# A banded attention and FFN kernel: one issue order for both phases, and shared DMA semaphores taken in written order

## The chip, the cores and the metric

One core of a Trainium2 chip runs the kernel. The metric is the device time of one execution in microseconds (us), the median of several executions. Engines are named as the profile names them: PE is TensorE (PEld its weight loads), DVE is VectorE, ACT is ScalarE, POOL is GpSimd, SP is SyncE; ACTq and SPq are the transfers that ACT and SP issue.

## What is computed

The reference, cut to what matters (q, k and v are 8 batches x 8 heads x 576 rows x 64, all float32):

```python
scores = (q @ k.T) / sqrt(64)              # per batch and head
scores = where((0 <= i - j) & (i - j < 64), scores, -1e9)
attn = softmax(scores)
x = (attn @ v)                             # heads side by side: 4608 x 512
h = x @ w_in                               # 512 x 2048
out = maximum(0.01 * h, h) @ w_out         # 2048 x 512
```

## The kernel before

**Tiling.** Attention goes through units of 64 query rows against a band of keys, four units of a group in a bank. A visit `s` (L369) is 64 small matmuls that make scores, a visit `o` (L458 in the first part, L829 later) multiplies the weights by v. Between them stand a mask (DVE L428, L755, ACT L415, L761), a maximum over the row (POOL L423, L770, L773), a subtraction and an exponential (DVE L777, ACT L444, L781) and the normalisation (DVE L477). `t` (L484) turns the normalised block `y` round on PE, so that the FFN can use it as x. Every float32 matrix of the FFN is split into a high and a low part, and a product is three matmuls (high by high, high by low, low by high) of 128x512.

**Two phases.** The first phase is written by hand as a string of step names, ORDER. A name is a kind and a number: `raw` fetches a weight block, `bits`, `sign`, `abs`, `clamp`, `join`, `chi` and `rest` (L302 to L342) take it into high and low parts, partly on DVE, partly on ACT; S, E, P, N, sub, exp, V, sm, rec, y, T, H, L are attention; M, lk, gh, gl, W are the FFN (`h` L522, `acc` L558); X is an idle filler; q, k and v are loads. The main program loops over these names and calls each step at once. What remains is then planned: `op`, `load` and `bulk` append each operation of the late part to a list, `plan`, and `arrange` calls them in the order of a table of plan numbers, PLACES. The late part finishes chunks 0 to 2 directly (`h` L1038, `acc` L1047) and then does three slices with seven products in place of eight: `m` (L1243) is a product, `z` (L1309) the second half's. For them, sums of weight blocks are made (`fetch` L1149, DVE L1152, ACT L1155) and kept in HBM by `keep` (L1162, `w_sums` and `w_first`); results leave PSUM by ACT `put` (L1249), DVE `add` (L1252) and ACT `leaky` (L1255). `pxa`, `pxb`, `pfew`, `pspare` and `p` are buffers used by turns. POOL fetches the kept sums back (L1227). Names of weight blocks that come late stand after a bar in ORDER.

**Loads.** `load_q` and `load_k` (L255, L259), `load_v` (L266) and `load_qk` (L262) bring 256 KB to 512 KB each for one attention group. SP and ACT issue transfers; POOL issues its own by another kind of queue. SP's and ACT's transfers share eight hardware semaphores (DMAHW0 to DMAHW7), one to a transfer and by turns. So a transfer that takes a semaphore can only be issued when the transfer that took it eight places before has landed, and the engine that issues stands still until then, with all that is behind it in its own order.

**Order.** At the end of the program each instruction is tied to the one before it on the same engine, so that each engine's order is the written one. Between engines only data and semaphores decide. Which transfer takes which semaphore follows the order in which the transfers of both engines come up when the semaphores are given out; nothing ties it to the written order across SP and ACT.

```python
order, late = ORDER.split("|")
for name in order.split():
    step(name)()
...
for n in map(int, PLACES.split()):
    assert placed.issuperset(a["n"] for a in plan[n]["after"])
    yield plan[n]["fn"]
```

Of the kernel before, what the change touches and what calls it, by code (L numbers as in the profile page):

```python
# [61 lines left out]
PLACES = """  # L62
30 1 7 40 0 38 39 5 2 31 3 10 32 17 41 42 43 44 13 33 34 4 6 45 35 36 9 51 8 12 11 14 15 52 48 16 18 23 49 53 19 59 20 149 50 22 54 21 162
25 55 24 26 56 27 62 28 60 29 63 37 521 46 150 520 61 152 64 69 151 57 65 47 66 155 67 73 153 154 156 164 70 158 71 74 531 165 177 72 530
75 80 522 81 524 76 157 166 167 159 77 68 78 525 523 84 160 526 85 163 82 527 86 91 87 83 170 161 529 88 58 528 89 168 179 532 169 534 173
95 202 181 92 180 96 171 533 172 97 102 182 93 101 98 174 192 535 99 94 536 197 175 193 194 541 540 103 100 537 106 104 185 198 176 105
538 107 183 222 539 108 186 117 184 196 109 178 188 195 204 114 110 206 226 111 205 119 115 543 189 210 217 120 542 544 218 207 116 121
219 127 118 122 187 545 211 203 123 551 190 124 546 130 550 128 131 547 208 191 132 549 199 133 209 134 129 548 220 213 212 221 228 140
146 136 141 135 138 275 142 229 200 143 552 276 147 139 231 137 241 214 554 277 283 555 553 278 251 215 230 556 279 148 280 561 242 246
243 560 223 232 216 234 286 145 227 112 224 557 284 287 235 245 201 288 294 244 289 225 559 233 290 285 271 237 291 247 297 558 295 253  # L70
562 266 236 564 565 298 267 239 603 296 268 238 255 299 125 305 254 300 563 301 566 302 256 240 308 306 567 570 252 309 307 259 571 568
248 310 569 316 257 269 605 270 260 258 79 311 249 607 262 261 312 627 313 319 317 618 318 320 264 606 263 581 619 620 321 327 322 580 250
323 272 324 265 608 273 315 330 572 573 331 611 609 332 341 274 304 333 610 126 612 328 623 343 614 329 622 613 344 621 334 303 624 574
335 642 647 582 345 643 338 575 644 616 339 615 346 342 576 347 353 584 629 617 348 314 650 630 349 340 632 350 577 356 354 631 578 357
355 635 358 372 585 583 359 628 625 579 360 633 646 361 645 636 634 375 626 366 604 638 637 368 652 373 364 665 376 362 590 653 640 377
639 383 666 374 144 378 586 282 654 379 380 648 386 384 658 641 674 385 667 387 649 293 655 90 388 393 670 1196 591 656 659 657 389 587
390 391 661 396 394 1195 395 689 397 660 592 1186 593 671 690 398 663 662 651 399 668 694 669 400 402 691 401 676 403 664 405 678 697 367
589 594 1185 677 682 406 404 595 407 411 679 408 409 683 410 1198 684 680 414 1141 412 687 588 675 415 596 416 672 681 699 712 413 693 685
692 113 417 700 721 688 420 418 701 419 713 1197 714 423 421 325 705 686 422 424 1188 1187 673 1199 363 425 702 429 426 1205 1143 427 695
428 706 696 432 336 703 707 292 597 1206 715 433 430 716 736 710 704 434 435 717 1200 1189 737 431 708 738 711 436 718 281 437 741 438 441  # L80
1142 1144 1201 709 723 599 1152 439 365 442 725 724 729 443 447 1207 444 1190 445 440 726 1191 446 719 698 450 722 1145 740 448 730 739
451 369 727 731 744 734 452 745 456 449 746 453 757 720 728 454 326 1153 455 598 1209 459 457 1202 458 732 460 1203 461 465 462 1150 1155
1156 749 1208 1204 742 735 1154 743 1151 1161 748 463 747 464 1146 337 1210 1192 468 1148 1265 466 1211 1162 469 602 1147 733 470 467 474
471 1149 600 472 753 1163 750 473 754 477 601 1157 759 755 478 774 760 756 475 352 751 761 479 762 752 764 480 381 476 763 481 371 1212
1159 482 483 486 484 765 767 1225 1158 1168 487 1170 1274 768 488 1164 769 1160 489 1193 485 772 1174 776 492 370 351 490 791 777 1226 491
1171 778 1166 495 1167 758 773 779 781 493 496 780 1165 1169 1172 497 494 784 501 498 1173 766 499 500 782 770 504 502 785 505 1194 503
1179 506 1175 1181 507 1177 783 1178 508 1286 771 1176 793 1180 1183 512 775 509 1184 513 510 514 511 1182 515 516 1266 518 1295 1228 816
1227 1268 796 1267 797 1270 1269 1216 801 794 1272 1271 795 808 798 786 809 1275 802 810 1215 517 1273 1213 392 1277 1276 787 799 1214 800
813 1229 838 1278 1230 1307 818 788 789 1279 819 841 820 1284 1217 1219 1287 1280 1285 1316 790 1218 1231 382 823 821 1289 811 803 1288
519 812 822 1291 1290 1281 826 1293 1220 824 1221 804 1292 1296 1235 827 1283 1298 1294 1222 833 843 1297 806 805 1223 1224 1299 1303 825  # L90
844 866 1232 1236 1305 845 1328 1304 807 1308 792 1306 848 834 1310 1309 835 1340 1312 1311 829 846 1314 1313 847 1317 1245 1315 1419 849
851 1322 1246 828 1237 830 1318 1324 1323 831 814 1234 1233 1326 1325 858 850 1329 1327 1349 832 1331 1330 836 1361 859 1247 860 1333 852
854 1332 837 1321 1335 1256 1319 1249 1248 863 1334 1370 1336 868 1250 1341 891 869 853 1239 1255 1240 1343 871 856 817 883 855 842 1345
815 1342 1251 1344 1347 1346 870 1302 873 1350 1348 1238 1352 839 1351 1382 884 872 861 885 1354 1337 1353 876 857 862 1257 1359 1258 1259
1355 1362 1360 1391 874 1356 1260 1364 1252 1261 1300 877 1366 1339 1262 875 1368 1254 1363 879 878 1365 888 1264 1367 1369 893 1358 1420
908 1263 1371 894 881 880 1253 1241 864 1373 896 887 895 840 909 1375 1378 886 1374 1372 898 882 1380 1379 865 910 897 1383 916 1403 1381
1415 1385 1384 901 1387 1416 1421 1389 1388 1386 1377 899 1392 1242 900 1301 1397 904 1393 1282 1390 1244 1243 1399 902 867 1461 1398 913
903 889 905 1376 906 918 892 912 1396 911 1401 919 890 1400 920 1404 1402 933 1430 907 923 1406 1405 921 1408 1407 934 1417 935 922 1410
1424 924 926 941 1425 1422 1412 1441 1320 1411 1423 1338 1409 925 927 1394 1426 929 914 1428 1427 1357 1413 1429 938 1433 1450 1467 930
1439 961 936 1434 1431 917 1579 956 937 1395 957 915 1440 1432 928 931 1435 1444 1414 1436 1472 1442 1448 1475 1445 932 958 1464 1443 1531  # L100
1446 1449 1453 1418 1447 939 1451 1462 1487 1454 960 959 1584 1452 1463 1437 979 1586 1455 1580 1438 1537 1468 1456 980 1585 984 1473 1459
1496 1582 1469 943 1590 981 1465 940 1457 1478 1466 1474 1470 1479 1583 1581 1548 1471 1480 1476 1485 1508 962 1477 1486 982 983 1481 1490
963 1505 1597 1482 1491 1595 1591 1488 1494 1519 1511 1489 1592 1495 1492 1499 1484 1596 1493 1587 1593 1497 1500 1506 1534 1588 1483 1498
985 1594 1501 986 1507 1599 1502 1512 1516 1509 1513 1545 1517 1600 1601 1510 1460 1522 1514 1518 1523 1515 1598 1589 1520 1612 1559 1532
1458 1524 1521 1503 1525 1538 1504 1533 964 1526 1542 1535 1568 1539 1543 1536 1527 1540 1544 1549 1617 1602 1541 1603 1550 1546 1623 1557
1613 1604 1606 1547 1615 1558 1551 1562 1616 1529 1619 1552 1607 1530 1528 1614 1560 1632 1566 1555 1605 1563 1561 1618 1564 1571 1567
1621 1565 1572 1610 1569 1644 1553 1608 1620 1554 1611 1570 1556 1609 1573 1622 1574 945 942 944 949 1624 1575 1577 1576 966 946 1625 1578
950 1626 987 951 1653 1628 1627 954 1630 1629 947 1633 1631 948 967 952 1635 1634 968 1637 1636 1642 1638 1665 953 955 972 1645 1643 965
989 1646 969 1647 1010 973 991 1649 1648 995 990 1651 1650 1674 970 1654 1652 992 974 1656 971 1002 1003 1686 1661 1657 975 1663 1662 1639
1007 1664 1655 977 976 1030 1004 1012 1666 993 1033 988 1013 1777 978 1668 1667 1015 1670 1669 1005 1014 1672 1671 996 994 1018 1675 1673  # L110
1680 1698 998 1682 1681 1677 1684 1025 1683 997 1676 1035 1707 999 1006 1000 1687 1036 1056 1037 1689 1026 1685 1027 1016 1691 1688 1001
# [85 lines left out]
def band_attention_ffn(ctx: ExitStack, tc: tile.TileContext, qk, vW, vL, w_in, w_out, eye_mask, out, outT):  # L197
# [415 lines left out]
    def step(name):  # L613
        kind = name.rstrip("0123456789")
        return partial(acts[kind], int(name[len(kind) :]))

    order, late = ORDER.split("|")
    for name in order.split():
        step(name)()
    prev = jobs[-1]  # L620


    plan = []

# [951 lines left out]
```

## Time and profile before

| what | us |
|---|---|
| three runs | 838.98, 838.88, 843.11 |
| median | 838.98 |
| span of the profiled execution | 841.2 |
| PE busy in it | 829.1 (99%) |
| DVE busy | 630.8 (75%) |
| ACT busy | 369.7 (44%) |
| POOL busy | 381.5 (45%) |
| DMA, mean over the span | 268 GB/s |

The profiled execution has no time of its own beside its span of 841.2 us, and that span is 2.2 us above the median of the runs. "Busy" of PE counts a matmul from its start to a modelled end, so a PE that is busy all the time can still be slowed by its clock. The clock column (PEclk) is the granted TensorE clock as a share of full speed, 2.4 GHz.

### The profile page before, as it was taken

The page shows a single profiled execution, that of the slowest core. Times are in us where ns is not written, and L with a number is a line of the kernel's source. Part 1 is how long each engine was busy: PE and PEld are TensorE (multiplying, and loading weights), DVE is VectorE, ACT ScalarE, POOL GpSimd, SP SyncE. Part 2 cuts the span into 40 slices and gives each one's busy share as a digit, 9 for nine tenths or more (in the row PEclk, how much of TensorE's full clock was granted, in tenths as well). Part 3 has the DMA queues.
Part 4 walks back from the last instruction along what each step waited for, and adds up shares of the span by engine and source line. Part 5 has one row for each costly group of instructions (what it writes and reads, how often), then busy time and mean ns, then how long its engine had stood idle before and what let it go on. Part 6 is the DMA issues. An engine that isn't in the chain of part 4 may idle for free.

```text
span 841.2 us, 16743 instructions
## 1 busy us (share of the span) xinstructions
PE 829.1 (99%) x6733; PEld 678.1 (81%) x6733; DVE 630.8 (75%) x912; ACT 369.7 (44%) x599; POOL 381.5 (45%) x216
## 2 busy tenths in 40 slices
PE   8999999999999999989999999999999999999997
PEld 5777888888888888868888888887888888888886
DVE  6999897777766698667888987559799863366773
ACT  4666555344423355243564442233545422325432
POOL 5332000897867747687672116797941111111110
PEclk9999999999999999999999999999999999999999
DMA  9886866987887899999999798899998996677772
GB/s 327 278 276 209 310 223 225 319 287 259 277 295 251 271 342 379 365 299 359 361 321 308 224 316 251 255 282 241 261 278 243 317 257 184 190 197 200 212 200 89
DMA packets 131005, 225.75 MB, mean 268 GB/s; under 512 B 15856, under 2 KB 53744, under 8 KB 130928
## 3 DMA queue, kind: packets, MB, share of 16 engines
q0 software_dynamic: 53568, 88.09, 38.8%
q10 hardware_dynamic: 36608, 78.26, 27.6%
q1 hardware_dynamic: 40752, 58.34, 21.7%
q8 instruction: 53, 0.87, 0.4%
q14 instruction: 24, 0.20, 0.1%
HBM read 167.28 MB, written 57.26 MB: 267 GB/s over the span
## 4 chain that ended last, share of the span: by engine, by line
PE 89%; DMA 5%; DVE 3%; issue 1%; ACT 1%; POOL 0%; DVEq 0%; ACTq 0%
PE z L1309 27%; PE m L1243 25%; PE acc L1047 11%; PE h L1038 11%; PE acc L558 4%; PE s L369 4%; PE h L522 4%; PE o L829 3%; DMA w_sums<-pspare 2%; DMA qk<-qk 1%; DMA raw<-w_in 1%; DMA raw<-w_out 1%; DMA w_single<-w 1%; PE o L458 0%; DVE raw L321 0%
## 5 line engine op out<-in xcount | busy, mean ns | idle before, releaser
L1243 PE MATMUL m<-pfew,p 128*128 128x512 f32 x720 | 171.6, 394 | 3.0 <-ACT pxa L1249 2.5
L1243 PEld LDWEIGHTS m<-pfew,p 128*128 128x128 f32 x720 | 135.5, 189 | 32.5 <-ACT pxa L1249 2.9
L1309 PE MATMUL z<-gs,p 128*128 128x512 f32 (+1 forms) x360 | 86.0, 387 | 0.0
L1047 PE MATMUL acc<-p,gs 128*128 128x512 f32 x324 | 80.7, 393 | 0.0
L1309 PE MATMUL z<-pxa,p 128*128 128x512 f32 x324 | 78.5, 391 | 0.0
L1309 PEld LDWEIGHTS z<-gs,p 128*128 128x128 f32 x360 | 67.3, 188 | 13.9
L1309 PE MATMUL z<-pspare,p 128*128 128x512 f32 x324 | 78.0, 389 | 0.0
L1252 DVE TENSOR_TENSOR pxa<-m,pxa 128x512 f32<-128x512 f32 x60 | 41.2, 688 | 48.5 <-PE m L1243 43.6
L770 POOL PARTITION_ALL_REDUCE g<-late_f x20 | 36.3, 1842 | 86.6 <-DVE late_f L755 71.5
L1227 POOL DMA_DIRECT2D p<-w_first x42 | 31.7, 755 | 93.7 <-PE m L1243 51.6
L1309 PEld LDWEIGHTS z<-pspare,p 128*128 128x128 f32 x324 | 60.7, 188 | 12.6
L1309 PEld LDWEIGHTS z<-pxa,p 128*128 128x128 f32 x324 | 60.5, 188 | 12.9 <-issue 0.2
L1243 PE MATMUL m<-pxb,p 128*128 128x512 f32 x288 | 70.6, 391 | 0.0
L1047 PEld LDWEIGHTS acc<-p,gs 128*128 128x128 f32 x324 | 60.0, 188 | 12.8
L773 POOL PARTITION_ALL_REDUCE late_o<-late_f x20 | 65.2, 3274 | 9.6 <-ACT late_f L781 7.4
L773 POOL PARTITION_ALL_REDUCE late_o<-e x18 | 61.5, 3432 | 16.6 <-issue 7.9
L1252 DVE TENSOR_TENSOR p<-m,pxa 128x512 f32<-128x512 f32 x60 | 40.7, 687 | 36.6 <-PE m L1243 35.9
L773 POOL PARTITION_ALL_REDUCE late_o<-late_e x18 | 59.3, 3321 | 10.6 <-ACT late_e L781 6.0
L1243 PEld LDWEIGHTS m<-pxb,p 128*128 128x128 f32 x288 | 53.8, 188 | 11.4
L1227 POOL DMA_DIRECT2D p<-w_sums x24 | 18.0, 749 | 93.1 <-PE z L1309 76.8
L1038 PE MATMUL h<-pxa,p 128*128 128x512 f32 x228 | 55.9, 392 | 0.0
L1038 PEld LDWEIGHTS h<-pxa,p 128*128 128x128 f32 x228 | 42.4, 188 | 9.0
(201 smaller groups left out, 1600.5 us busy)
## 6 DMA issues: line engine op xcount, KB each, us to landing
p<-w_first POOLq DMA_DIRECT2D x42, 1024.0 KB, 7.0
p<-w_sums POOLq DMA_DIRECT2D x24, 1024.0 KB, 6.7
p<-w_second POOLq DMA_DIRECT2D x18, 1024.0 KB, 6.9
qk<-qk ACTq DMA_DIRECT2D x26, 512.0 KB, 6.2
w_single<-w ACTq DMA_DIRECT2D x32, 256.0 KB, 3.7
raw<-w_out ACTq DMA_DIRECT2D x15, 512.0 KB, 4.5
raw<-w_in ACTq DMA_DIRECT2D x14, 512.0 KB, 4.3
more_v<-vL ACTq DMA_DIRECT2D x14, 512.0 KB, 6.0
```

The source lines that it names most:

```text
L369: nc.tensor.matmul(ps[j][t, c : c + QB], k[i][s, p], q[s, w, p], start=not begun and (not more or (w, p) == (0, 0)), stop=not begun and no ...
L522: nc.tensor.matmul(ps, a[:, k, :], b[:, k, part], start=n == 0, stop=n == len(terms) - 1)
L558: nc.tensor.matmul(acc[c, i], a[:, ts], b, start=begin and n == 0, stop=end and n == 2)
L770: nc.gpsimd.partition_all_reduce(most_of(j), e_of(m)[:, j], P, ReduceOp.max)
L773: nc.gpsimd.partition_all_reduce(sum_of(j), e_of(m)[:, j], P, ReduceOp.add)
L829: nc.tensor.matmul(ps[64 * j : 64 * j + 64, c : c + QB], v[:, 2 * p + j], e_of(m)[:, j, c : c + QB], start=True, stop=True,)
L1038: nc.tensor.matmul(ps, a[:, k, :], b[:, k], start=i == 0, stop=i == len(terms) - 1)
L1047: nc.tensor.matmul(acc[c, i], a[:, i * P : (i + 1) * P], b, start=begin and k == 0, stop=n in ends and k == 2)
L1227: nc.gpsimd.dma_start(to, of, max_dma_last_dim=2048)
L1243: nc.tensor.matmul(tiles[b], w[:, 256 * i + 128 * kt : 256 * i + 128 * kt + 128], x_part(OF_X[k], j, kt), start=begin and c == 0, stop=c = ...
L1252: nc.vector.tensor_tensor(to(), tiles[b], x(), ALU.add)
L1309: nc.tensor.matmul(tiles[b + i][:, cut], a, x[:, cut], start=begin and f == first and c == 0, stop=f == half - 1 and c == 2, skip_group_ch ...
```

## The change

PLACES and ORDER become one string, ORDER, in which names (first phase) and plan numbers (late part) stand together; `arrange` yields a step for a name and a planned operation for a number. The names of late weight blocks move to a string of their own, LATE_WEIGHTS. Buffers of g in the planned part are counted on from the number of jobs. At the end of the program, a transfer of SP or ACT whose forerunner among all transfers of these two is on the other engine gets an order dependency on it, one that adds no semaphore wait of its own: with it the shared semaphores are taken in the written order. The rest is the order itself: the first phase's names and the numbers stand in another sequence. Each engine has the same multiset of instructions as before (PE 5003, DVE 914, ACT 785, POOL 221, SP 293 in the program); no load, matmul or copy comes in or goes. Line numbers of the changed file are some 3 to 7 lower.

```diff
-PLACES = """
-30 1 7 40 0 38 39 5 2 31 3 10 32 17 41 42 43 44 13 33 34 4 6 45 35 36 9 51 8 12 11 14 15 52 48 16 18 23 49 53 19 59 20 149 50 22 54 21 162
...
+ORDER = """
+X6 raw0 S0 X2 E1 E0 X1 q1 bits0 sign0 Z1 Z0 k1 abs0 raw1 P1 v0 S1 N1 bits1 E2 P0 clamp0 q2 sign1 join0 exp1 k2 P2 raw2 abs1 N0 V1 exp0 V0
...
-ORDER = """
-raw0 k1 X6 S0 q1 E1 X2 Z1 E0 bits0 sign0 Z0 P1 S1 abs0 v0 P0 raw1 clamp0 join0 N1 E3 bits1 exp1 N0 q2 P3 V1 exp0 sign1
...
+LATE_WEIGHTS = """
...
-    order, late = ORDER.split("|")
-    for name in order.split():
-        step(name)()
     prev = jobs[-1]
+    turns_late = counter(len(jobs))
...
     def arrange():
         placed = set()
-        for n in map(int, PLACES.split()):
+        for word in ORDER.split():
+            if not word.isdigit():
+                yield step(word)
+                continue
+            n = int(word)
             assert placed.issuperset(a["n"] for a in plan[n]["after"])
...
-    pair_at = [pairs_of_g[next(turns) % 2] for _ in walk]
+    pair_at = [pairs_of_g[next(turns_late) % 2] for _ in walk]
...
+    order_of_issue = mybir.DependencyInfo(mybir.DependencyClass.NoSync, mybir.DependencyReason.SCHED_ONLY)
+    issued, transfer = {}, None
     for ins in nc.cur_bb.bb.instructions:
...
+        issued[ins.engine] = ins
+        if type(ins).__name__ == "InstDMACopy" and ins.engine != mybir.EngineType.Pool:
+            if transfer is not None and transfer.engine != ins.engine:
+                tc.add_manual_dep(ins, transfer.name, order_of_issue, reason="order of transfers")
+            transfer = ins
```

**ACT in the late part, at the start of the first slice of seven products.** `m0_0_0` and `m0_1_0` are the first two banks of products, and `COPY pxa1 <- m0_1_0` (`put`) empties the second. ACT's order before, with what each instruction waits for (DMAHW6_49 is shared semaphore 6, PE_49 a count on PE):

```order
440 L1149 DMA p14_25_2962<-w_single_94 128x512 [waits DMAHW2_49]
441 L761 COPY late_e_1764<-s22_0_3758 128x512 [waits DVE_49]
442 L788 ACTIVATE late_c0_1770<-late_c0_1770 128x8 [waits DMAHW4_49]
443 L781 ACTIVATE e_76<-e_76 128x512
444 L1149 DMA p14_25_2962<-w_single_94 128x512
445 L1162 DMA w_sums_97<-pspare_18_1772 512x1x256 [waits DMAHW6_49]
446 L1255 ACTIVATE p9_38_3880<-m0_0_0_3813 128x512 [waits PE_49]
447 L1162 DMA w_sums_97<-pspare_18_1772 512x1x256 [waits DMAHW1_49]
448 L781 ACTIVATE late_e_1764<-late_e_1764 128x512 [waits DVE_49]
449 L262 DMA qk0_83<-qk 128x1024 [waits DMAHW7_49,DMAHW6_49,PE_49]
450 L761 COPY late_f_1765<-s23_0_3924 128x512 [waits DVE_49,Pool_49]
451 L1249 COPY pxa1_37_3834<-m0_1_0_3969 128x512 [waits PE_49]
```

Between the `put` of `m0_0_0` (row 438, just above these) and that of `m0_1_0` (row 451) ACT issues five transfers, and the load of qk0 waits on semaphore 6, which the transfer of row 445 took. The same place after the change:

```order
438 L257 DMA qk1_84<-qk 128x1024 [waits DMAHW4_49]
439 L1067 COPY pxa0_35_3842<-acc2_3_2853 128x512
440 L1246 COPY pxa1_36_3847<-m0_0_0_3830 128x512 [waits PE_49]
441 L1159 DMA w_sums_97<-pspare_19_1832 512x1x256 [waits DMAHW6_49]
442 L778 ACTIVATE e_76<-e_76 128x512 x2
443 L785 ACTIVATE late_c0_1783<-late_c0_1783 128x8 [waits DMAHW7_49,DMAHW1_49]
444 L1252 ACTIVATE p9_38_3906<-m0_0_0_3830 128x512 [waits PE_49]
445 L778 ACTIVATE late_e_1777<-late_e_1777 128x512 [waits DVE_49]
446 L257 DMA qk0_83<-qk 128x1024 [waits PE_49]
447 L758 COPY late_f_1778<-s23_0_3910 128x512 [waits DVE_49,Pool_49]
448 L1246 COPY pxa1_36_3847<-m0_1_0_3948 128x512 [waits PE_49]
```

Two transfers are left between the two `put`s; the two loads of `p14` and the first `w_sums` have gone ahead of the first `put` (rows 430, 433 and 425 of ACT's order), and qk0 waits for PE alone.

**PE in the first phase, at the turn of the block `t4`.** Before (`h_3_0` is the last product of an FFN block, 12 matmuls of which the last four rows are shown):

```order
325 L522 MATMUL h_3_0_795<-pxa_13_324,pfew_85 128x512
326 L522 MATMUL h_3_0_795<-pxa_12_323,pfew_85 128x512 x2
327 L522 MATMUL h_3_0_795<-pxa_13_324,pfew_85 128x512
328 L522 MATMUL h_3_0_795<-pxa_12_323,pfew_85 128x512
329 L484 MATMUL t_809<-unit,y_753 128x128 [waits DVE_49,PE_49]
330 L484 MATMUL t_809<-unit,y_753 128x128 x3
331 L458 MATMUL o_814<-p_0_77,e 64x65 [waits DMAHW4_49,PE_49,Activation_49]
```

and now:

```order
312 L553 MATMUL acc_2_0_770<-pfew_85,gs_81 128x512 x3
313 L553 MATMUL acc_3_0_774<-pfew_85,gs_81 128x512 x3
314 L479 MATMUL t_795<-unit,y_732 128x128 [waits DVE_49,PE_49]
315 L479 MATMUL t_795<-unit,y_732 128x128 x3
316 L517 MATMUL h_3_0_802<-pxa_12_379,pfew_85 128x512 [waits Activation_49]
317 L517 MATMUL h_3_0_802<-pxa_13_380,pfew_85 128x512
```

The turn `t4` and its wait for DVE stand 12 matmuls earlier, ahead of `h_3_0`.

**SP at the start.** Before:

```order
3 L302 DMA raw0_105<-w_in 128x1024
4 L259 DMA qk1_84<-qk 128x512
5 L255 DMA qk1_84<-qk 128x512
6 L266 DMA v_72<-vW 128x2x520
7 L302 DMA raw1_199<-w_out 128x1024 [waits DMAHW0_49]
8 L255 DMA p14_1_78<-qk 128x512 [waits DMAHW1_49]
```

and now:

```order
3 L297 DMA raw0_114<-w_in 128x1024
4 L250 DMA qk1_84<-qk 128x512
5 L254 DMA qk1_84<-qk 128x512
6 L297 DMA raw1_164<-w_out 128x1024
7 L261 DMA v_72<-vW 128x2x520 [waits DMAHW0_49]
8 L250 DMA p14_1_78<-qk 128x512 [waits DMAHW1_49]
```

The second weight block's load and the first load of v have changed places, and with them the wait on semaphore 0, which the first load of qk took.

## Rows read from the trace of the kernel before

**Rows 1.** The page: span, and busy time of each engine.
```profile
span 841.2 us, 16743 instructions
PE 829.1 (99%) x6733; PEld 678.1 (81%) x6733; DVE 630.8 (75%) x912; ACT 369.7 (44%) x599; POOL 381.5 (45%) x216
```

**Rows 2.** Stretches: length, busy us (count) by engine, PEclk, DMA share, GB/s.
```profile
0.00:20.00 20.00, 17.55 (x311) 11.21 (x315) 12.52 (x27) 9.68 (x17) 10.93 (x10) 1.00 0.92 331
20.00:40.00 20.00, 18.92 (x319) 15.28 (x315) 18.44 (x45) 13.05 (x27) 9.14 (x5) 1.00 0.85 270
40.00:60.00 20.00, 19.11 (x226) 15.55 (x215) 19.05 (x42) 12.48 (x24) 4.57 (x2) 1.00 0.86 281
...
200.00:300.00 100.00, 100.00 (x1013) 81.83 (x1012) 68.45 (x101) 39.12 (x71) 75.45 (x30) 1.00 0.83 273
...
340.00:368.00 28.00, 25.03 (x275) 20.21 (x274) 17.45 (x26) 9.55 (x18) 19.37 (x11) 0.94 1.03 330
```

**Rows 3.** PE's waits over the span: us in total, times, longest.
```profile
PE m L1243 <- ACT pxa L1249: 2.5, 1, 2.5
PE t L484 <- DVE y L477: 1.4, 2, 0.7
```

**Rows 4.** ACT's timeline: start, us, instruction, idle before and its releaser.
```profile
349.19 0.53 ACTq L1162 DMA_DIRECT2D w_sums<-pspare  x1
...
358.42 0.34 ACTq L262 DMA_DIRECT2D qk<-qk  x1
358.86 0.58 ACT L761 COPY late_f<-s 128x512 f32<-128x512 f32 x1 [8.46 <-DMA w_sums<-pspare]
359.34 0.59 ACT L1249 COPY pxa<-m 128x512 f32<-128x512 f32 x1
```

**Rows 5.** The chain of waits from 335 to 368: start, us, what.
```profile
343.71 14.64 DMA w_sums<-pspare
...
358.42 7.89 DMA qk<-qk
```

**Rows 6.** PE's timeline from 346 to 368.
```profile
350.40 3.02 PE L1243 MATMUL m<-pxb,p 128*128 128x512 f32 x12
353.25 4.24 PE L1243 MATMUL m<-pfew,p 128*128 128x512 f32 x18
359.98 4.60 PE L1243 MATMUL m<-pfew,p 128*128 128x512 f32 x12 [2.49 <-ACT pxa L1249]
...
366.45 0.36 PE L369 MATMUL s<-qk,qk 64*64 64x64 f32 x3 [0.48 <-DMA qk<-qk]
```

**Rows 7.** Stretches of 10 us, columns as in rows 2.
```profile
290.00:300.00 10.00, 10.00 (x82) 8.30 (x75) 9.14 (x14) 4.07 (x7) 6.91 (x4) 1.00 0.85 253
...
350.00:360.00 10.00, 7.51 (x63) 5.90 (x54) 3.13 (x7) 1.53 (x4) 4.07 (x3) 1.00 1.19 372
360.00:370.00 10.00, 9.52 (x92) 7.55 (x93) 9.09 (x11) 5.63 (x10) 9.35 (x4) 0.83 0.71 232
```

**Rows 8.** DMA issues: engine, count, KB each, median us to landing.
```profile
w_sums<-pspare ACTq DMA_DIRECT2D x4, 512.0 KB, 10.2
```

**Rows 9.** DVE's waits from 20 to 80: us in total, times, longest.
```profile
DVE raw L317 <- DMA raw<-w_out: 1.3, 1, 1.3
DVE w L334 <- DMA w_single<-w: 0.9, 1, 0.9
```

**Rows 10.** Line L1290: duration in ns as min/median/max, first and last start.
```profile
L1290 DVE TENSOR_TENSOR gs<-p,gs x30: 1172/1222/3868, 405.9 to 829.8; 128x1024 fp32r<-128x1024 f32 x30
```

**Rows 11.** Timelines of DVE and of PE around 578.
```profile
575.68 3.87 DVE L1290 TENSOR_TENSOR gs<-p,gs 128x1024 fp32r<-128x1024 f32 x1
...
580.21 1.67 PE L1243 MATMUL m<-pfew,p 128*128 128x512 f32 x6 [0.47 <-DVE pxa L1252]
```

**Rows 12.** SP's and PE's timelines at the start; time to landing of the tile v's loads.
```profile
3.06 0.67 SPq L266 DMA_DIRECT2D v<-vW  x1
...
12.15 1.03 PE L458 MATMUL o<-v,e 128*64 128x65 f32 x18
...
DMA to landing us min/median/max: 5.9/6.4/6.9
```

## What was predicted before the changed kernel ran

> **What bounds the kernel now.** I read the page first. PE is busy for 829.1 of 841.2 us [rows 1], so the kernel is bound by PE, and with no matmul added or taken the change can only gain or lose the 12.1 us in which PE does nothing, plus what a low clock adds. Next I read PE's busy time by stretches. Of the 12.1 us, 2.45 lie in the first 20 us, 1.08 from 20 to 40, 0.89 from 40 to 60, and 2.97 from 340 to 368; from 200 to 300 there is none [rows 2]. Most of the rest is a tail after the last matmul, which the order of the middle does not touch. So there are two places to look at.
>
> The larger is at 360. PE's longest single wait is for ACT's copy of a finished bank [rows 3]. ACT's timeline says why the copy was late: ACT sat idle for 8.46 us until 358.86, and in its order there stood a transfer, the load of qk, issued at 358.42 [rows 4]. The order places of ACT show that it waits for shared semaphore 6, which the transfer of `w_sums` had taken. That transfer was issued at 343.71 and landed 14.64 us later, at 358.35, and the load of qk, late by that, landed 7.89 us after its own issue [rows 5]; the same transfer's median is 10.2 us [rows 8]. PE pays three times [rows 6]: 2.49 us of idle time before 359.98; the 12 matmuls that follow take 4.60 us where 12 with the clock up took 3.02, so 1.58 more; and 0.48 us at 366.45, where the scores wait for the qk that was issued late. The granted clock of 360 to 370 is 0.83 [rows 7], which fits matmuls at the lower of the two levels (1.2 GHz) for some microseconds after PE stood idle. The sum is 2.49 + 1.58 + 0.48 = 4.55 us.
>
> The smaller place is the first phase, where DVE is busy for 18.44 and 19.05 of 20 us [rows 2] and PE twice waits 0.7 us for DVE's `y` [rows 3].
>
> **The change, part by part.**
>
> *The order at 360.* Between the two `put`s ACT now issues two transfers where it issued five. The load of qk waits for PE alone, since its semaphore's last taker has already been waited for by an instruction ahead of it. The `put` of `m0_1_0` also goes ahead of a second copy. So the wait of 8.46 us goes, and with it all three payments: -4.55. What is late next there is the one `w_sums` left (row 441), which waits on semaphore 6. I place each transfer by PE's work at which it stands, 12 matmuls being 2.85 us from one start to the next [rows 6]: before, the transfer that had to land for qk stood 4.6 us of PE work ahead of it, now that for `w_sums` stands 9.2 us ahead. A transfer of this kind takes 10.2 us as the median [rows 8], so ACT may still stand for about 1 us; PE is 5.9 us of matmuls (the rows at 350.40 and 353.25) ahead of needing the copy, which hides it. Bounds: nothing left to pay (4.55 gained), or the same long landing of 14.64 us against 9.2, a stand of 5.4 us, which the 5.9 us just cover. I take -4.55, and keep as the lower bound a gain of only the last 0.48.
>
> *How much moves at that place.* The DMA engines are full there: 372 GB/s at a share of 1.19 from 350 to 360, against 253 at 0.85 from 290 to 300 [rows 7]. By the sizes of the transfers and their places in both orders I estimate that PE's work from 300 to 340 has 17.2 MB asked for in it before, and 14.5 after, since some loads go earlier. That is 430 against 362 GB/s over 40 us, so before it asks for more than the 372 that were moved, and now for less. By that the long landing of 14.64 us should fall as well. The Trainium skill (DMA: Bandwidth & Descriptors, "Issuing engines are not separate DMA queues") says that transfers started by different engines run on the same 16 DMA engines and interleave, so that spreading them over engines saves the issuing time alone. By that rule alone the new order would not shorten any landing, and the sum here would be 0; the trace speaks for it in so far as the rate is at its highest exactly where the transfer is slow.
>
> *The other transfers moved.* They go into PE's work from 140 to 300, where 172 transfers of SP and ACT stand after and 164 before. DMA moves 273 GB/s at a share of 0.83 from 200 to 300 and PE loses nothing there [rows 2]. I cost it at 0; its cover is the slack of POOL's ring loads and of ACT (39 of 100 us busy). If that is gone, the price is a stall like the one at 360, 4.55 us each.
>
> *Semaphores in written order.* The dependency adds no wait that an engine sees; it changes which transfer is eight places ahead. By itself I put it at 0, with bounds of one stall on either side (-4.55 where it undoes one, +4.55 where it makes one), since each of the engines' orders holds dozens of such waits.
>
> *The first phase.* The raw weight loads go ahead by some microseconds, so DVE's waits for them, 1.3 and 0.9 us [rows 9], can go; in stretches where DVE is the feeder that is up to 2.2 us. The wait of `t4` stands 12 matmuls earlier, 2.85 us less time for DVE, but DVE has about as much less work ahead of that `y`, so I take the two to cancel; the bounds are no wait (-0.7) or a wait longer by 1.5. The first v is issued after a weight load: at about 4.6 in place of 3.06, and with 6.9 us to landing at most it lands at 11.5, before its reader at 12.15 [rows 12]: 0. Together I take -0.5, from -2.0 to +1.5.
>
> *At 579* an addition on DVE took 3.87 us where the median is 1.22 [rows 10, 11], while POOL worked, and PE waited 0.47 us. In another order the two fall otherwise: -0.47, bounds -0.47 and +0.5 for one such meeting elsewhere.
>
> **The sum.** 841.2 - 4.55 - 0.5 - 0.47 = 835.7 us for an execution like the profiled one. The median of the runs, 838.98, is 2.2 below its span. Either those runs had the same stall and less of something else (then 838.98 - 5.5 = 833.5), or they lacked part of the stall, whose length hangs on when a transfer lands (then 835.7 stays). The trace can't tell which, so I take the middle: **834.6 us**, 0.52% below the median. About 0.5% is what a measurement of this kernel can tell from no change, which puts the bounds at 834.8 and 843.2.
>
> **The rivals.**
>
> 1. *The stall is hardly in the median.* Had the transfer landed in its median of 10.2 us [rows 8] instead of 14.64, qk would have gone out 4.4 us earlier and PE's idle time of 2.49 would not exist; the runs at 838.9 would then have little to give. The gain is then 1 to 3 us: 836 to 838. For it speaks the 2.2 us between span and median; against it that DMA is as full at 350 in every execution of the same order.
>
> 2. *The pile-up is one of bandwidth and stays.* The DMA engines are full from 300 to 360, the transfers merely change places, and another of them is late by as much: 838.98 give or take 1.5. Against it speak the 14.5 MB for 17.2. The Trainium skill's page "DMA: Bandwidth & Descriptors", in the section named above, is the rule that would give this.
>
> 3. *A new wait on the other side.* In PE's work from 140 to 300 I count 84 of 109 SP transfers under 8 us behind the transfer that had their semaphore, before 62 of 103, and 41 of 63 of ACT, before 35 of 61. Score visits stand closer, 6.5 us at the closest where it was 8.6, and DVE and ACT evict h on the same engines. When a transfer there takes over 8 us to land, ACT stands ahead of an activation that PE's next product needs; it decides when ACT stands longer than the 5 or 6 us of matmuls that PE has in hand. Two stalls of 4.55 us with the gain as forecast give 834.6 + 9.1 = 843.7, slower. Against it: the rate of 273 GB/s there leaves room to the 372 that were moved at the fullest place.
>
> 4. *The first phase gains much.* DVE's 2.2 us of waits go and 1.6 of the 2.0 us of PE's idle time from 20 to 60, beside the stall: 2.2 + 1.6 = 3.8, of which the forecast has 0.5, so 834.6 - 3.3 = 831.3.
>
> **How the numbers follow.** My forecast (833 to 836) has 0.44, rival 1 has 0.17, rival 2 has 0.11, rival 3 has 0.12, rival 4 has 0.16. The range leaves out rival 3 and the far half of rival 4: 831 to 841.5. Faster by over 0.5% (under 834.8) is rival 4 and a little over half of the forecast, whose centre stands 0.2 us under the bound: 0.16 + 0.25 = 0.41. Slower by over 0.5% is rival 3: 0.12. The rest, 0.47, is within 0.5%.
>
> **What the profile of the changed kernel would show.** Right: no wait of PE `m` for ACT's `put` at the first seven-product slice, no ACT idle time over 3 us ahead of it, granted clock 1.00 in every stretch from 340 on, PE busy in all of 340 to 368 but for 0.1 us after visits. The first phase: DVE waits for `raw` and `w_single` under 1 us, PE idle from 20 to 60 between 0 and 3 us. Wrong: a stretch between 140 and 300 where PE idles and ACT stands behind a transfer (rival 3); a wait for `put` or `qk` of over 2 us still there, with a landing over 14 us (rival 2); or all as said, and the time yet near 838 (rival 1).

## The result, and the profile after

The changed kernel takes 851.32 us (847.23 to 853.32, four runs), the kernel before 839.5 (838.88 to 843.11, four runs): 1.0124 times as long, 95% interval 1.0086 to 1.0161. The profiled execution took 850.91 us and has a span of 849.1, so 1.8 us lie around a span. It is slower, on the other side of what was forecast and outside the range.

The page of the changed kernel:

```profile
span 849.1 us, 16713 instructions
...
PE 832.0 (98%) x6733; PEld 675.8 (80%) x6733; DVE 647.5 (76%) x912; ACT 369.0 (43%) x599; POOL 381.3 (45%) x216
```

PE is now idle for 17.1 us where it was for 12.1 [rows 1], and DVE is busy 16.7 us longer with the same instructions. Stretches, columns as in rows 2 (length, busy us and count of PE, PEld, DVE, ACT, POOL, then PEclk, DMA share, GB/s):

```profile
0.00:20.00 20.00, 16.85 (x284) 10.62 (x285) 13.23 (x25) 9.24 (x16) 10.17 (x9) 1.00 0.92 336
20.00:40.00 20.00, 18.80 (x288) 15.24 (x287) 19.44 (x45) 12.87 (x25) 10.06 (x5) 1.00 0.79 262
40.00:60.00 20.00, 20.00 (x258) 16.55 (x257) 19.54 (x44) 13.78 (x27) 3.83 (x2) 1.00 0.81 264
200.00:300.00 100.00, 100.00 (x1066) 81.88 (x1065) 73.29 (x99) 38.74 (x71) 74.99 (x30) 1.00 0.93 317
300.00:340.00 40.00, 38.44 (x339) 30.91 (x338) 30.45 (x47) 20.67 (x36) 22.72 (x11) 1.00 0.99 311
340.00:368.00 28.00, 27.10 (x346) 21.28 (x345) 23.91 (x35) 11.29 (x20) 23.51 (x13) 1.00 1.01 308
```

The stretch of the old stall has 0.90 us of idle time where it had 2.97, at full clock where it had 0.94 [rows 2]. The stretch from 200 to 300 is as full as before, though more is moved there (317 GB/s for 273). The loss is elsewhere. PE's waits from 100 us on, in us in total, times, longest:

```profile
PE acc L1044 <- DVE gs L1055: 1.5, 1, 1.5
PE z L1306 <- DVE pspare L1287: 1.1, 1, 1.1
PE m L1240 <- DMA p<-w_first: 1.0, 1, 1.0
PE z L1306 <- DVE pxa L1287: 1.0, 1, 1.0
PE m L1240 <- DVE p L1249: 0.8, 2, 0.6
PE z L1306 <- ACT p L1252: 0.8, 1, 0.8
PE h L1035 <- DVE gs L1055: 0.7, 1, 0.7
```

The row that led before, `m` waiting 2.5 us for ACT's `pxa` [rows 3], is gone; twelve waits of at most 1.5 us have come, 8.5 us together with the four rows not shown. They are spread from 196 to 703 us. To see what may lie behind them, take the pair at 508 and 512 (`pspare` and `pxa`), DVE's timeline:

```profile
500.89 1.22 DVE L1287 TENSOR_TENSOR gs<-p,gs 128x1024 fp32r<-128x1024 f32 x1
507.77 0.42 DVE L990 TENSOR_TENSOR g<-e 128x256 f32<-128x256 f32 x1 [5.67 <-DMA e<-x_rows]
508.12 1.22 DVE L1287 TENSOR_TENSOR pspare<-pxa,pspare 128x1024 fp32r<-128x1024 f32 x1
...
512.13 1.22 DVE L1287 TENSOR_TENSOR pxa<-p,pxa 128x1024 fp32r<-128x1024 f32 x1
```

and the chain of waits there:

```profile
493.50 0.61 DVE late_n L851
...
494.12 5.27 DMA x_rows<-late_n
...
499.96 7.72 DMA e<-x_rows
```

DVE finishes a normalised block (`late_n`), SP stores it to HBM, SP loads it back as x, and DVE's first step on that x stands in DVE's order ahead of `pspare` and `pxa`, for which PE waits. The way through HBM takes from 494.1 to 507.7; DVE had come to the reader at 502.1 and stood 5.67 us. At 339 it is similar: DVE stands 3.47 us behind `p<-x_rows` until 334.68, and PE waits 1.5 us for the `gs` that DVE makes later. Other things that attention sends through HBM are waited for too. DVE's and ACT's waits of that kind from 100 us on, changed kernel:

```profile
DVE late_n L851 <- DMA late_r<-rows: 11.7, 6, 4.0
DVE g L990 <- DMA e<-x_rows: 5.7, 1, 5.7
DVE p L990 <- DMA p<-x_rows: 4.4, 2, 3.5
ACT late_c L785 <- DMA late_c<-late_o: 18.9, 7, 6.2
ACT pfew L1009 <- DMA late_n<-x_rows: 5.8, 1, 5.8
```

Before, of these rows DVE has only 0.6 us for `late_r` and ACT 0.4 for `late_c`. All of DVE's and ACT's waits for a DMA from 100 us on, added over such rows, are 40.3 us before (8.5 of them the stall at 360) and 82.6 after.

### The profile page after: what moved, and what is told of

Same layout as the page of the kernel before. It is cut to its first block, busy times and chain, and to the rows that moved or that the text cites. A ratio compares the mean times of both kernels' runs of the same rounds, so it can differ in the third digit from the quotient of the medians.

```text
span 849.1 us, 16713 instructions
## 1 busy us (share of the span) xinstructions
PE 832.0 (98%) x6733; PEld 675.8 (80%) x6733; DVE 647.5 (76%) x912; ACT 369.0 (43%) x599; POOL 381.3 (45%) x216
## 4 chain that ended last, share of the span: by engine, by line
PE 71%; DMA 13%; DVE 12%; issue 2%; ACT 1%; POOL 1%; SPq 0%; ACTq 0%; DVEq 0%; POOLq 0%
PE m L1240 22%; PE z L1306 20%; PE h L1035 8%; PE acc L1044 7%; PE acc L553 4%; PE h L517 4%; PE s L364 3%; PE o L826 3%; DMA raw<-w_out 2%; DMA p<-w_sums 1%; DMA p<-w_first 1%; DMA qk<-qk 1%; DMA x_rows<-late_n 1%; DMA p<-x_rows 1%; DMA v<-vL 1%
## 5 line engine op out<-in xcount | busy, mean ns | idle before, releaser
L767 POOL PARTITION_ALL_REDUCE g<-late_f x20 | 39.3, 1993 | 85.7 <-DVE late_f L752 76.7
L1224 POOL DMA_DIRECT2D p<-w_first x42 | 31.7, 755 | 97.5 <-PE m L1240 52.6
L770 POOL PARTITION_ALL_REDUCE late_o<-e x18 | 59.2, 3304 | 15.1 <-ACT e L778 9.1
L1224 POOL DMA_DIRECT2D p<-w_sums x24 | 18.0, 750 | 95.3 <-PE z L1306 86.1
```

The source lines that it names most:

```text
L767: nc.gpsimd.partition_all_reduce(most_of(j), e_of(m)[:, j], P, ReduceOp.max)
L770: nc.gpsimd.partition_all_reduce(sum_of(j), e_of(m)[:, j], P, ReduceOp.add)
L1224: nc.gpsimd.dma_start(to, of, max_dma_last_dim=2048)
```

## The experiments

### Which part: four crossings

`pin_only` has the old orders and only the new dependency; `new_order_unpinned` is the changed kernel without it; the other two cross the phases, with the dependency in.

```diff
# new_order_unpinned
-            if transfer is not None and transfer.engine != ins.engine:
-                tc.add_manual_dep(ins, transfer.name, order_of_issue, reason="order of transfers")
# new_first_old_late: names as changed, numbers as in PLACES of before
 ORDER = """
 X6 raw0 S0 X2 E1 E0 X1 q1 bits0 sign0 Z1 Z0 k1 abs0 raw1 P1 v0 S1 N1 bits1
...
+30 1 7 40 0 38 39 5 2 31 3 10 32 17 41 42 43 44 13 33 34 4 6 45 35 36 9
...
# pin_only: names and numbers as before; old_first_new_late: names as before, numbers as changed
```

> The orders of before, and only the dependency that makes SP's and ACT's transfers take the shared semaphores in written order. Theory 'late order' (the new order of the late part makes the new stalls, the semaphores do nothing): 837 to 841 us. Rival 'semaphores' (the loss comes from which transfer waits for which): 847 to 853. My prediction's term of 0 with bounds of one stall: 835 to 843.

> The new order of both phases without that dependency. Theory 'late order': as the changed kernel, 847 to 853 us, since each engine's order is the same. Rival 'semaphores': back to 837 to 841.

> The new order of the first phase's names, the late part in its old order, semaphores in written order. Theory 'late order': 837 to 841 us, with PE's idle time from 20 to 60 under 1.2 us as in the changed kernel's profile (1.20, before 1.97). Rival 'first phase' (what the first phase leaves for later makes the stalls): 847 to 853.

> The old order of the first phase, the late part in the new order, semaphores in written order. Theory 'late order': 847 to 853 us, with PE waiting for DVE and ACT at slice products after 420 as in the changed kernel. Rival 'first phase': 837 to 841.

| kernel | us, median | ratio to before, 95% |
|---|---|---|
| pin_only | 842.19 | 1.0041 (1.0018 to 1.0063) |
| new_first_old_late | 841.13 | 1.0037 (1.0017 to 1.0058) |
| old_first_new_late | 852.88 | 1.0176 (1.0148 to 1.0205) |
| new_order_unpinned | 866.71 | 1.0337 (1.0307 to 1.0367) |

With the dependency in, the loss comes with the late part's new order: with it 851 to 853 us, without it 841 to 842, whichever first phase stands ahead. The semaphores are no small matter either, against the theory that they do nothing: the dependency costs 0.4% in the old order and gives back 15 us (866.71 to 851.32, 2.1% by the ratios) in the new one.

In the old order the trace of `pin_only` shows both sides of it: PE's waits, two stretches, and SP's issue of the v that PE waits for, in `pin_only` (L260) and in the kernel before (L266).

```profile
PE o L452 <- DMA v<-vW: 3.1, 1, 3.1
```

```profile
20.00:40.00 20.00, 15.74 (x254) 13.05 (x254) 15.80 (x42) 11.06 (x22) 7.65 (x4) 0.91 0.77 256
...
340.00:368.00 28.00, 28.00 (x325) 23.18 (x317) 22.74 (x34) 11.42 (x22) 22.04 (x12) 1.00 1.14 369
```

```profile
19.03 0.55 SPq L260 DMA_DIRECT2D v<-vW  x1
```

```profile
13.64 0.55 SPq L266 DMA_DIRECT2D v<-vW  x1
```

From 340 to 368 PE has no idle time: with the semaphores in written order the load of qk waits on another transfer (a `p<-w_single` that landed at 351.63), and the stall of 4.55 us does not exist. In the first phase, though, v's turn now falls on the semaphore of a load of `w_single` that lands at 18.98, so v is issued 5.4 us later and PE waits 3.1 us for it, at a granted clock of 0.91. With the new first phase that wait is gone (`new_first_old_late`: 18.89 us busy from 20 to 40). That stretch differs from execution to execution, however: of the 14 profiles with the new first phase nine have 18.8 to 19.0 us there and five 17.1 to 17.7.

### Taking attention's waits away

All transfers stay and each engine's order stays (two memsets come in with the first edit); what changes is what the readers read.

```diff
# sums_no_wait: the sums land beside the columns that are read, the product doesn't read the rows
-        nc.sync.dma_start(later["c"][m % 2][64 * j : 64 * j + 64], ...)
+        nc.sync.dma_start(later["landing"][m % 2][64 * j : 64 * j + 64], ...)
-        r = sum_of(0) if direct(m) else later["r"]
+        r = turned(sum_of(0)) if direct(m) else by_unit(done_of(m))
# x_no_round_trip: x is loaded from an input
-                xt_of()[0].rearrange(...), x_rows[m : m + 2].rearrange("i p c -> p i c")
+                xt_of()[0].rearrange(...), qk[0:2, :, 0].rearrange("i p a b c -> p i (a b c)")
# neither_waits: both; neither_waits_old_order: both, on pin_only
```

> The changed kernel in its own order, all transfers kept, but nobody reads what the sums send through HBM: the sums' transfer lands in a column of its own, the guard reads a constant, and the product multiplies by its own tile (it leaves out the division by the sum). Theory 'round trips': DVE's waits for late_r (11.7 us) and ACT's for late_c (18.9 us) go, and 3 to 7 us of the 12 with them, 844 to 848. Rival 'DVE and POOL in each other's way, or semaphores': 849 to 853, since no instruction and no transfer is gone.

> The changed kernel in its own order, but the loads of x for the slices read an input that is in HBM from the start, so that they don't wait for x's store to land (it leaves out that the slices compute with x). Theory 'round trips': DVE's wait of 5.7 us for x at 507 and the one of 3.5 at 334 shorten, and with them the stalls of PE at 337 to 346 and 507 to 512 (4.9 us together): 845 to 849. Rival: 849 to 853.

> Both edits on the changed kernel. Theory 'round trips': 839 to 844 us, nearly all of the loss back. Rival: 848 to 853.

> Both edits on the orders of before with semaphores in written order (842.19 us as such). Theory 'round trips': 839 to 843, since readers there start 4 to 6 us after the landing as the median and little waits. Were it to gain as much as the changed kernel does by the same edits, the theory falls: the gain would be that of doing less.

| kernel | us, median | ratio to before, 95% | PE's waits after 100 us, in its profile |
|---|---|---|---|
| changed | 851.32 | 1.0124 (1.0086 to 1.0161) | 8.5 in 12 |
| sums_no_wait | 849.94 | 1.0099 (1.0073 to 1.0124) | 7.7 in 8 |
| x_no_round_trip | 851.52 | 1.0123 (1.0067 to 1.0178) | 4.8 in 7 |
| neither_waits | 846.57 | 1.0063 (1.0035 to 1.0091) | 4.7 in 7 |
| pin_only | 842.19 | 1.0041 (1.0018 to 1.0063) | 0.5 in 1 |
| neither_waits_old_order | 840.71 | 1.0000 (0.9974 to 1.0025) | 1.7 in 3 |

By the point estimates both edits together give back half of the loss, 1.24% to 0.63%. By the times alone that is not shown: the intervals touch, and the old order gains 0.4% by the same edits.

The edit on the sums does what it should: DVE's 11.7 us for `late_r` and ACT's 18.9 for `late_c` are gone, and yet the time hardly moves (1.0099 for 1.0124, within the intervals). So these 30.6 us of waits on DVE and ACT cost the kernel little that can be measured.

The edit on x does only half of what was expected of it. The stall at 339 is gone in its profile, but the pair at 508 and 512 is still there (0.88 and 0.99 us), since DVE stands nearly as long as before:

```profile
503.81 0.43 DVE L990 TENSOR_TENSOR g<-e 128x256 f32<-128x256 f32 x1 [5.00 <-DMA e<-qk]
```

The reason is a buffer: ahead of the load into `e` SP has the load into `late_n`, and `late_n` is what the store `x_rows<-late_n` reads. So whatever the loads fetch, the first can only go out when the store has landed (here at 495.52, the store at 495.43), and the second stands behind it. In `neither_waits` it is the same: the store lands at 498.05, the load into `late_n` is issued at 498.13, the one into `e` at 498.63, DVE stands 4.36 us, and PE waits 0.24 and 1.00 us. That DVE's wait for x makes this pair is therefore read from the trace, and no run has taken it away.

In the profiles PE's waits fall from 8.5 to 4.7 us by both edits in the new order; in the old one there is nothing to take (0.5 and 1.7). The gain of the control lies in the first phase, which the edits don't touch: its v is issued as late (18.43) but lands after 5.2 us instead of 7.1, and PE waits 0.8 us for it in place of 3.1. But these are one execution each: `x_no_round_trip` was profiled in its fastest (847.27) and has 4.8 us of waits with no gain in the median, and the changed kernel itself has an execution of 847.23. So attention's waits are a part of the loss as far as the profiles go, some 4 of 8 us of PE's waits, and how large a part is not shown.

At 432 ACT's timeline in `neither_waits` shows a third kind of wait:

```profile
421.97 0.52 ACTq L1162 DMA_DIRECT2D w_sums<-pspare  x1
...
432.26 1.04 ACT L1286 CAST pspare<-p 128x1024 fp32r<-128x1024 f32 x1 [6.53 <-DMA w_sums<-pspare]
```

This is not the shared semaphore of rows 4, since a copy waits here and no transfer. The copy writes `pspare`, which the `w_sums` store of 421.97 reads, and it can start only when that store has landed, 10.27 us after its issue; PE's `z` waits 1.6 us for what ACT does next. The changed kernel has the same wait (5.66 us until 432.10; its row names `late_c`'s transfer, which landed then too, but the copy waits for the stores). Before, the same copy came at 430.64, 10.3 us after the store's issue, and the store had landed in 5.9 us.

### Moving readers and transfers

In each, the named steps move in ORDER by up to so many us of PE work, never past one that they need or that needs them.

```diff
# old_readers_earlier, in ORDER of pin_only: 134 moves of guard_of, product_of, sub, high_of up to 6 us earlier; one of them (1054 is a product)
-1063 1102 1731 1730 1087
+1063 1102 1731 1054 1730 1087
...
-1067 1743 1742 1054 1745 1744
+1067 1743 1742 1745 1744
# old_readers_later, in ORDER of pin_only: the same steps up to 3 us later
-1067 1743 1742 1054 1745 1744 1074 1075
+1067 1743 1742 1745 1744 1054 1074 1075
# new_readers_later, in ORDER of the change: the same steps up to 5 us later
-1088 1761 1741 1054 1082 1743
+1088 1761 1741 1082 1743
...
+1094 1095 1782 1054 1099 1779
# new_act_transfers_later, in ORDER of the change: fetch, keep, load_qk, load_v up to 4 us later; one of them (757 is a load of qk)
-447 446 729 757 450 730
+447 446 729 450 730
...
+719 1202 370 757 453 727
```

> The orders of before with semaphores in written order (842.19 us as such), and one thing moved: the instructions that read what attention sent through HBM (guard, product, first steps of x) stand up to 6 us of PE work earlier, not past what they need. From the issue of the sums' rows to their reader the order then has 5.8 us of PE work as the median in place of 11.1, as close as in the changed kernel (6.3). Theory 'readers too close': 847 to 854 us, DVE and ACT waiting for DMA 60 us or more together after 100 (before 40, changed 83). Rival 'ACT behind shared semaphores alone': 840 to 844.

> Control: the same base, the same instructions moved later by up to 3 us, not past what needs them. Theory 'readers too close': 839 to 843, nothing to gain where the median reader starts 6 us after the landing. If moving alone costs: over 846.

> The changed kernel (851.3 us) with the same kind of instruction moved up to 5 us later, not past what needs them; no other order changes. Theory 'readers too close': 843 to 848. Rival 'ACT behind shared semaphores alone': 849 to 853.

> The changed kernel with ACT's own transfers (loads of qk, v and weights, stores of the sums of weights) up to 4 us of PE work later in ACT's order, not past what needs them, so that each stands further behind the landing that its semaphore waits for, and more of ACT's copies go ahead. Theory 'ACT behind shared semaphores': 844 to 848, ACT's waits for DMA under 35 us (changed 57.8). Theory 'readers too close' alone: 849 to 854.

Measured: 879.23 (ratio 1.0470, 1.0415 to 1.0524), 846.72 (1.0078, 1.0041 to 1.0114), 877.76 (1.0444, 1.0384 to 1.0504) and 887.30 us (1.0561, 1.0508 to 1.0614).

The first says that readers close to their transfers are enough to lose, and by more than expected: DVE's and ACT's waits for a DMA come to 108 us after 100. Its rows:

```profile
DVE late_n L850 <- DMA late_r<-rows: 26.2, 8, 8.1
DVE p L989 <- DMA p<-x_rows: 12.5, 2, 7.1
...
PE m L1239 <- DVE pxa L1248: 11.3, 4, 4.3
```

The control, though, stands 0.4% above `pin_only` by moving alone (the intervals overlap), and the two repairs of the new order miss by far: they cost 26 and 36 us. What is moved later hands its result on later, and what needs that now stands instead. ACT's waits did fall as expected in the last (24.4 us for 57.8), while DVE's rose to 50.1. So these two refute nothing about the cause, and show that an order like this can't be mended by moving one kind of instruction.

The same holds for four earlier crossings inside the late part: ORDER was merged anew from both orders, each step sorted by the PE work ahead of it, one class of steps by the place that it had before, the rest by the place that it has after. Of `load_qk` 757 and `product_of` 1054, `attention_at_old_places` has:

```diff
-1189 447 446 729 757 450 730 451
...
+449 746 1208 454 757 720 728 281
...
-1677 1088 1761 1741 1054 1082 1743
...
+1057 1066 1067 1743 1054 1742 1745 1074
```

> The changed kernel, in whose late part all attention operations (visits, masks, maxima, exponentials, sums, the sums' and x's ways through HBM, their readers) stand at the places they had before, counted in PE work; weights and FFN stay in the new order. Theory 'round trips' (the new order puts the readers of what attention sends through HBM too close behind the transfer, so DVE, ACT and POOL stand in their orders): 838 to 844 us. Rival 'FFN and weights' (the stalls come from the new order of DVE's, ACT's and POOL's other work): 847 to 853.

> The complement: weights and FFN of the late part at the places of before, attention where the changed kernel has it. Theory 'round trips': 846 to 855 us, DVE waiting for rows of the sums and for x by over 10 us together. Rival 'FFN and weights': 838 to 844.

> The changed kernel with only attention's last part at the old places: from the transfers of the sums on (reciprocal, product, x to HBM and back, x's split); scores, masks, maxima and exponentials stay where the change put them. Theory 'round trips': 839 to 846 us, most of the loss gone, DVE's waits for rows and x under 5 us. Rival 'front' (scores and maxima closer together fill DVE and POOL): 847 to 853.

> The complement: only attention's last part where the changed kernel has it, all else of the late part at the old places. Theory 'round trips': 846 to 856 us. Rival 'front': 838 to 844.

They took 900.68, 895.28, 892.78 and 880.71 us, 5 to 7% above the kernel before: both of each pair of complements lose, so they tell nothing apart. Two orders, each made to fit as a whole, do not fit when one is laid over the other.

### What is left, and the version that the runs point to

```diff
# neither_waits_no_reduces, on neither_waits
-        nc.gpsimd.partition_all_reduce(most_of(j), e_of(m)[:, j], P, ReduceOp.max)
+        nc.gpsimd.tensor_copy(most_of(j)[:, :8], e_of(m)[:, j, :8])
-        nc.gpsimd.partition_all_reduce(sum_of(j), e_of(m)[:, j], P, ReduceOp.add)
+        nc.gpsimd.tensor_copy(sum_of(j)[:, :8], e_of(m)[:, j, :8])
# new_first_old_late_unpinned: new_first_old_late without the dependency
```

> The kernel neither_waits (846.57 us) with POOL's all-reduces of the late part (maxima and sums) left out, a copy of eight columns in the place of each. It is for the rest of the loss, some 6 us against neither_waits_old_order (840.71). Theory 'DVE slowed while POOL reduces' (DVE's instructions take 73 us over their forms' medians in the changed order, 55 in the old one, nearly all of it with an all-reduce running): 836 to 841 us, and that excess under 25. Rival 'ACT behind shared semaphores': 844 to 848, since every transfer is still there in the same order.

> The version that the runs point to: the first phase's new order, the old order of the late part, and no dependency on the semaphores' order. The first phase's new order gave 1.1 us (842.19 to 841.13), the missing dependency 3.6 (842.19 to 838.54). If both add up: 837 to 838.5 us; if the semaphores that fall out of it are as the written order's: 840 to 842.

The first took 851.32 us (1.0168, 1.0128 to 1.0208). The theory that DVE's slowness beside POOL's all-reduces is the rest finds no support: that slowness went (what DVE's instructions take above the median of their line and shape fell from some 73 to 9 us) and PE's waits rose to 8.5 us. It isn't ruled out by this, since the edit shifts when everything behind POOL happens, and shifts alone have cost much in the runs above. The second took 845.33 us (1.0070, 1.0046 to 1.0094), so the two gains don't add up, and no version here beats the kernel before. With the new first phase and the old late part the dependency thus saves 0.3% (1.0070 to 1.0037), where with the old first phase it costs 0.4%. The profile has the old stall again, PE's waits from 300 to 400:

```profile
PE s L363 <- DMA qk<-qk: 2.0, 1, 2.0
PE m L1239 <- ACT pxa L1245: 1.4, 1, 1.4
```

Without the dependency the stall of rows 4 to 6 comes back, at the same place: the load of qk goes out at 362.27, when the transfer of `w_sums` that had its semaphore has landed (362.20, 13.2 us after its issue).

One more possible cause is in the traces, and was not tried alone. POOL's loads of the kept sums (L1224) went out one by one in the old order, 5.4 us apart; in the new one neighbours are swapped at 11 places (3 in the old one), so that a load whose buffer is free stands behind one whose buffer is not, and then both go at once. POOL's timeline in the changed kernel:

```profile
691.88 1.49 POOL L1224 DMA_DIRECT2D p<-w_first  x2 [10.14 <-PE z L1306]
702.76 1.48 POOL L1224 DMA_DIRECT2D p<-w_first  x2 [9.39 <-PE m L1240]
```

and in `new_first_old_late`, at the same place:

```profile
686.76 0.74 POOL L1223 DMA_DIRECT2D p<-w_first  x1 [4.59 <-PE m L1239]
692.31 0.74 POOL L1223 DMA_DIRECT2D p<-w_first  x1 [4.80 <-PE m L1239]
```

Of the two of 691.88, one landed 10.77 us after its issue, and PE waited 0.99 us for it at 703.44. From 380 us on there are 11 such pairs after and 2 in `new_first_old_late`. PE's rows put 1.4 us on these loads (1.0 on `w_first`, 0.4 on `w_sums`).

## Why the prediction was wrong

**The step that failed.** The sum priced what becomes of the old stalls and put all else that the late part's new order does at 0: "the other transfers moved", with the slack of POOL's ring loads and of ACT as cover. The crossings show what that order costs: 10 us (851.32 us for 841.13, ratio 1.0124 for 1.0037, with the same first phase and the same dependency), where the whole sum had 5.5 to gain. The sum had no term for the distance from a transfer to the instruction that needs it landed, as a reader or as the next writer of its buffer. By PE's planned work the product stood 11 us behind the issue of the sums' rows as the median before, and stands 4 to 6 behind it now; for the loads of x it is about half of what it was. Measured from the landing, 25 of the changed kernel's 120 transfers of these kinds have a reader that starts within 0.5 us, so one that was waiting; in `pin_only` 5. The slack of ACT was no cover, since an engine that is idle for half of the time still stands in its order. And POOL's queue was not looked at: its loads changed places.

**Rival 3** had the right kind, ACT and DVE standing in their orders behind landings, and the wrong place: from 200 to 300 PE still loses nothing, so the cost of the traffic moved there was right.

**The stall at 360.** The mechanism was right and the change does remove it: no wait of `m` for the `put`, clock 1.00, PE busy 27.10 of 28 us. The base was wrong: the sum took 4.55 us off, and then off the median. In all runs an execution takes 1.7 to 1.9 us more than its span, so the one profiled, with 841.2, took about 843.0 us, as long as the slowest of the runs (843.11); those at 838.9 are 4 us shorter, about the stall. That they lack it was not seen in a trace; `new_first_old_late_unpinned`, too, shows the stall in a profile of the slowest of its six executions (848.43, the fastest 842.68). This was the premise of rival 1, which had 0.17.

**Semaphores in written order** were put at 0 with one stall on either side. Measured: with the old late part the dependency costs 0.4% or saves 0.3%, by the first phase that stands ahead, and in the new order it saves 15 us. The place where its dozens of waits fall decides, and the bound of one stall was too narrow by a factor of three.

**The first phase** at -0.5: PE's idle time from 20 to 60 is 1.20 us for 1.97, DVE's waits for weights went from 2.2 to 0.2 as said [rows 9], and the first 20 us lose 0.7 of it again. `new_first_old_late` stands 1.1 us under `pin_only`, which is the forecast's direction and is not clear of the intervals.

**At 579** nothing was gained: PE's start there is 0.78 us late, before 0.63 (spacing of the matmuls).

**What stays open.** In the profiles PE's waits after 100 us are 8.5 us in the changed kernel and 1.1 in `new_first_old_late`, 7.4 of the 10.7 us between the two spans; the rest is in gaps that the page counts as busy time of PE (832.0 for 827.9 us). That the late part's order makes the loss is shown. Which of its waits make it is not: attention's transfers are a part by the profiles of single executions, and for the rest the traces name ACT and SP behind shared semaphores, copies behind stores that still read their buffer, and POOL's paired loads. No run takes these apart.

## What to carry to other kernels

Where a whole order is new, look not only at what the old profile's stalls become: for every transfer compare the distance to its first reader, and to the next writer of the buffer that it reads, in both orders with the time that it flies, since an engine that comes there early stands with all that is behind it. Do the same for each queue of loads, and for the order in which buffers come free. Before a stall of the profiled execution is taken off the median, see where the profiled execution lies among the runs. And when an edit is to take a wait away, look in its trace whether the wait is gone: a load may wait for its buffer as well as for its data.

## What was not expected of the hardware

Leaving POOL's all-reduces out took DVE from 644.2 to 582.4 us busy and made the kernel no faster (846.57 to 851.32 us). And a dependency that adds no wait of its own, only another turn in eight semaphores, moved the time by 15 us (866.71 to 851.32).
